# Up-projection of three batches as seven block products with reloaded weights, down-projection in groups, and an order made by a list scheduler

## The chip, the cores and the metric

The kernel runs on one core of one Trainium2 chip. The time is device microseconds (us) of one execution. A core has TensorE (PE, matrix products, with its weight loads PEld counted apart), VectorE (DVE), ScalarE (ACT), GpSimd (POOL) and SyncE (SP, which here issues the transfers between DRAM and the on-chip memory SBUF). Products accumulate in PSUM, in banks of 128 x 512 f32. "L523" is a line of the kernel file.

## The reference

Four batches of 768 tokens, 8 heads of 64. Each query sees the keys less than 16 places away and 24 further keys, each the maximum of a block of 32 keys; their scores get log 32 added and their values are the blocks' means. The 512 numbers per token then go through a gated layer:

```
k_sum = k.reshape(B, H, nb, block, D).max(axis=3)
v_sum = v.reshape(B, H, nb, block, D).mean(axis=3)
...
x = attn_out.transpose(0, 2, 1, 3).reshape(B * S, H * D)      # 3072 x 512
g = x @ w_gate                                                # 512 x 1536
silu = g * (1.0 / (1.0 + np.exp(-g)))
val = x @ w_val
return (silu * val @ w_out).astype(np.float32)                # 1536 x 512
```

The three weight matrices come as float64 and are made into f32 on the chip by integer operations.

## The kernel before, in words

Tokens are worked on in 8 blocks k of 384 (batch k // 2, half k % 2). Attention is done in units (k, u), u = 0 to 3 being a pair of heads: scores on PE (L404), maximum on DVE (L419), exponential on ACT (L434), reciprocal on DVE (L454), scaling on POOL or DVE (L458), transposes on PE (L473), copies on ACT or DVE, values on PE (L497, tile xo). The unit's output, transposed, is 128 rows of x for 384 tokens, and `a_split` keeps it as a high part xh and a low part xl. Every f32 product of the gated layer is three matmuls in a fast format: low weight by high x, high weight by low x, high by high.

d_ff is cut into 12 slices j of 128. `m_up(k, j, nm)` makes gate or value of a block and slice: 4 row blocks u by 3 matmuls of 128 x 128 by 384 columns (L523). Then come silu on ACT (L530), the product with the value on DVE (L535, tile a), its high part ah on ACT (L159) and low part al on POOL or DVE (L155). `m_down(k, j)` is 9 matmuls of 512 columns (L574: 3 token tiles by 3 terms) into three PSUM banks, in which all 12 slices add up; after the last, three copies and stores (L581).

Weights: `w_load` (L175) fetches 1 MB of gate and value for a slice (gv) or 0.5 MB of w_out (o); `w_abs` (ACT, L184, the magnitude), `w_clamp`, `w_shift`, `w_sign` and `w_low` (DVE, L191 to L211) make f32 from the two words of a float64; `w_hi` (L159, ACT) and `w_lo` (L155, DVE or POOL) split it into the high and low part. The split weights of all 12 slices stay in SBUF to the end: every weight is loaded and decoded once.

The order of the work in blocks 0 and 1 is a text written by hand (`PROLOGUE`), with the engine of some steps in it; then a loop over (k, j) has gate, value and the down-projection of the slice before it, and attention of the next block is put at fixed places of the loop. On each engine, the instructions are chained in the order in which they were written.

## Time and profile before

| | us |
|---|---|
| three timed runs | 716.29, 717.04, 717.61 (median 717.04) |
| span of the profiled execution | 715.0 |
| PE busy in it | 704.7 (5062 instructions) |
| ACT, DVE, POOL busy | 322.2, 283.6, 140.1 |
| first gate product starts | 36.0 |
| last matmul ends | 711.25 |
| read from DRAM, written | 54.93 MB, 6.29 MB |

Group rows read: line, engine, operation, output<-inputs by the program's names, shape, count, then busy us in all and ns of one, then the engine's idle time ahead of them and who ended it. In the chain of waits each row is a start, a length, and the work or the wait that held the end at that time. A stretch's row has its length, the busy us and counts of PE, PEld, DVE, ACT and POOL, the granted clock of PE (1.00 is full speed), the busy share of the DMA engines and GB/s. A transfer's row has its size and the median us from issue to landing.

### The profile page before, as it was taken

To read this page: it belongs to the slowest core of one execution; us is meant where nothing else is said; L and a number is where in the kernel's file an instruction comes from. 1 tells how busy PE (TensorE), PEld (TensorE's weight loads), DVE (VectorE), ACT (ScalarE), POOL (GpSimd) and SP (SyncE) were. 2 spreads that over 40 slices of the span, in tenths; PEclk is the share of its full clock that TensorE was granted. 3 is DMA by queue.
4 is the path that set the end of the run, shared out by engine and by line. 5 is a ranking of instruction groups with operands and counts; after the bars stand their busy time and mean duration, and the time that the engine had idled before them with its cause. 6 is when DMAs were issued, how large, how long until landed. Compare 5 with 4: busy or idle time off the path is not lost.

```text
span 715.0 us, 12684 instructions
## 1 busy us (share of the span) xinstructions
PE 704.7 (99%) x5062; PEld 644.5 (90%) x5062; DVE 283.6 (40%) x832; ACT 322.2 (45%) x782; POOL 140.1 (20%) x155
## 2 busy tenths in 40 slices
PE   8899999999999999999999999999999999999997
PEld 7688999999889999999999999999999999999996
DVE  5999999926553212323422222232222321210001
ACT  5998444314774434544434444343444433421111
POOL 3232000002222122222122222122222212211111
PEclk9999999999999999999999999999999999999999
DMA  9999400407553101223213211111111200010001
GB/s 301 335 370 382 101 1 1 130 1 220 164 161 111 43 3 45 90 68 90 78 42 106 67 45 45 45 61 30 45 45 45 89 17 1 1 45 1 0 1 45
DMA packets 56523, 62.04 MB, mean 87 GB/s; under 512 B 24272, under 2 KB 46480, under 8 KB 55184
## 3 DMA queue, kind: packets, MB, share of 16 engines
q1 hardware_dynamic: 56464, 61.23, 27.4%
q8 instruction: 40, 0.66, 0.4%
q14 instruction: 19, 0.16, 0.1%
HBM read 54.93 MB, written 6.29 MB: 86 GB/s over the span
## 4 chain that ended last, share of the span: by engine, by line
PE 91%; DMA 4%; ACT 3%; issue 1%; SPq 0%; DVE 0%; ACTq 0%
PE v L523 28%; PE acc L574 27%; PE g L523 27%; PE xo L497 4%; PE sc L404 3%; PE pp L473 2%; DMA vw<-in_vP 1%; ACT p L434 1%; DMA raw_g<-in_wgv 1%; DMA kt<-in_kP 1%; ACT pt L159 0%; PE pv L373 0%; ACT L434 0%; ACT L530 0%; DVE m_gv L211 0%
## 5 line engine op out<-in xcount | busy, mean ns | idle before, releaser
L574 PE MATMUL acc<-w_o,ah 128*128 128x512 f32 x576 | 179.3, 392 | 0.0
L523 PE MATMUL v<-xh,w_gv 128*128 128x384 f32 x640 | 179.1, 340 | 0.0
L523 PE MATMUL g<-xh,w_gv 128*128 128x384 f32 x640 | 178.0, 339 | 0.0
L535 DVE TENSOR_TENSOR a<-v,a 128x384 f32<-128x384 f32 x96 | 53.3, 555 | 255.5 <-PE v L523 255.3
L155 POOL TENSOR_TENSOR al<-a,ah 128x384 fp32r<-128x384 f32 x79 | 81.1, 1027 | 264.5 <-ACT ah L159 264.5
L574 PEld LDWEIGHTS acc<-w_o,ah 128*128 128x128 f32 x576 | 108.0, 188 | 20.1
L523 PEld LDWEIGHTS v<-xh,w_gv 128*128 128x128 f32 x640 | 117.0, 188 | 3.1 <-issue 2.4
L523 PEld LDWEIGHTS g<-xh,w_gv 128*128 128x128 f32 x640 | 117.2, 188 | 2.9 <-issue 0.2
L574 PE MATMUL acc<-w_o,al 128*128 128x512 f32 x288 | 114.2, 396 | 0.0
L530 ACT ACTIVATE a<-g 128x384 f32<-128x384 f32 x96 | 47.1, 491 | 144.6 <-PE g L523 144.3
L523 PE MATMUL g<-xl,w_gv 128*128 128x384 f32 x320 | 107.8, 337 | 0.0
L523 PE MATMUL v<-xl,w_gv 128*128 128x384 f32 x320 | 107.7, 337 | 0.0
L159 ACT CAST ah<-a 128x384 fp32r<-128x384 f32 x92 | 46.9, 510 | 112.1 <-DVE a L535 112.1
L434 ACT ACTIVATE p<-p,nm 128x120 f32<-128x120 f32 x192 | 73.3, 383 | 1.1 <-DVE nm L419 0.7
L574 PEld LDWEIGHTS acc<-w_o,al 128*128 128x128 f32 x288 | 54.0, 188 | 10.1 <-issue 0.5
L523 PEld LDWEIGHTS g<-xl,w_gv 128*128 128x128 f32 x320 | 60.1, 188 | 2.5
L523 PEld LDWEIGHTS v<-xl,w_gv 128*128 128x128 f32 x320 | 60.1, 188 | 0.0
L530 ACT ACT_TABLE_LOAD x27 | 34.6, 1283 | 52.7 <-PE g L523 52.6
L458 POOL TENSOR_TENSOR p<-p,ri 128x720 f32<-128x720 f32 x26 | 36.2, 1391 | 98.5 <-DVE ri L454 98.0
L419 DVE CUSTOM_DVE_ANT_0 p<-sc,bias_sb 128x120 f32<-128x120 f32 x192 | 41.4, 276 | 0.7 <-PE sc L404 0.7
L523 PE MATMUL v<-xh,w_v 128*128 128x384 f32 x128 | 36.1, 342 | 0.7 <-DVE w_v L155 0.7
L523 PE MATMUL g<-xh,w_g 128*128 128x384 f32 x128 | 36.1, 343 | 0.0
(103 smaller groups left out, 721.3 us busy)
## 6 DMA issues: line engine op xcount, KB each, us to landing
raw_gv<-in_wgv SPq DMA_DIRECT2D x10, 1024.0 KB, 12.8
kw<-in_kP SPq DMA_DIRECT2D x28, 288.0 KB, 4.1
vw<-in_vP SPq DMA_DIRECT2D x28, 288.0 KB, 3.4
q<-in_qP SPq DMA_DIRECT2D x32, 192.0 KB, 3.6
raw_o<-in_wo SPq DMA_DIRECT2D x12, 512.0 KB, 11.5
out<-o SPq DMA_DIRECT2D x24, 256.0 KB, 2.3
stg<-in_kP SPq DMA_DIRECT2D x12, 400.0 KB, 3.7
vt<-in_vT SPq DMA_DIRECT2D x12, 384.0 KB, 3.5
```

Of the source, the lines that this page charges most:

```text
L155: (nc.vector if e == "d" else nc.gpsimd).tensor_tensor(out=out, in0=a, in1=b.bitcast(F32), op=ALU.subtract)
L159: nc.scalar.copy(out, in_)
L404: nc.tensor.matmul(sc[h][s * QT : (s + 1) * QT, c * KC : (c + 1) * KC], t["q"][hs, qs], t["kw"][hs, i, :], start=True, stop=True,)
L419: nc.vector.tensor_tensor_reduce(out=t["p"][:, i, :], in0=t["sc"][g][:, c * KC : (c + 1) * KC], in1=bias_sb[:, 0 if n == 0 else 2 if n == ...
L434: nc.scalar.activation(out=t["p"][:, i, :], in_=t["p"][:, i, :], func=AF.Exp, scale=-1.0, bias=t["nm"][:, i : i + 1], accum_out=t["sm"][:, ...
L458: (nc.vector if on == "d" else nc.gpsimd).tensor_tensor(out=p, in0=p, in1=ri.rearrange("p (n o) -> p n o", o=1).broadcast_to([P, NT, KC]), ...
L473: nc.tensor.transpose(ps[:KC, c * P : (c + 1) * P], U[k, u]["p"][:, g * NT // 2 + c, :], id_sb)
L497: nc.tensor.matmul(ps[hs, qs], vw, t["pt"][:, h, qs], start=True, stop=True)
L523: nc.tensor.matmul(ps[:, :TOK], w[:, cs], x, start=u == 0 and n == 0, stop=u == NP - 1 and n == 2)
L530: nc.scalar.activation(out=a, in_=A.pop(("g", k, j))[:, :TOK], func=AF.Silu)
L535: nc.vector.tensor_tensor(out=a, in0=ps[:, :TOK], in1=a, op=ALU.mult)
L574: nc.tensor.matmul(ACC[k][i], a[:, ts], w, start=j == 0 and n == 0, stop=j == NJ - 1 and n == 2)
```

## The change: seven block products, sums of weights, groups, and a scheduler

**Seven products.** For batches 1 to 3 the 512 rows of x are cut into two halves and the 768 tokens into two: blocks B11, B12, B21, B22 (row half, token half). For a slice j, gate weights are A11, A12 and value weights A21, A22 (by row half). With S1 = A21 + A22, S3 = A11 - A21, S2 = S1 - A11, S4 = A12 - S2 and T1 = B12 - B11, T2 = B22 - T1, T3 = B22 - B12, T4 = B21 - T2, the products P1 = A11 B11, P2 = A12 B21, P3 = S4 B22, P4 = A22 T4, P5 = S1 T1, P6 = S2 T2, P7 = S3 T3 give gate and value of both halves: gate of half 0 is P1 + P2; with U = P1 + P6, value of half 0 is U + P7 + P4, gate of half 1 is U + P5 + P3, value of half 1 is U + P5 + P7. Each product is 2 row blocks by 3 matmuls of 384 columns (`product`). P2, P4 and P3 are accumulated in the banks of P1, P7 and P5, after these have been copied or read (`s1`, `s7`, `v`); the rest is added on DVE and POOL.

**Operands.** `x_operands(b)` makes the seven high and low pairs from the batch's x: 8 subtractions, and a cast and a subtraction for each of 14 tiles. Attention units of batches 1 to 3 leave x as f32 (`a_keep`).

**Weights.** Batch 0 decodes the slices as before (`w_first`), now in a ring of four SBUF slots, and stores the split weights in DRAM (`wa{j}`, 1 MB each). In batches 1 to 3 `w_next` loads, for each slice, the three blocks that are used as they are, and the sums. In batch 1 the sums are made: the whole slice is loaded again, high and low added (`sm`), four sums made (`sums`), split (`sh`, `sl`), and stored (`ss{j}`); batches 2 and 3 load these. w_out stays in SBUF.

**Down-projection.** In groups of three slices: 9 matmuls for each and each of the six token tiles of a batch, in one bank; the group's sum is copied into (first group) or added to an f32 tile in SBUF (`part`), from which the output is stored.

**Order.** A `Plan` collects steps with the buffers that they read and write, the engines that can do them, and a cost for each. `order` simulates the engines, with a lag after PE and transfers, a price for a change of ACT's table, and gives each step an engine and a place; steps of attention go on a second list of PE's work, which is taken when the main one waits or when its time comes. The instructions are then chained in that order.

```diff
-    def m_up(k, j, nm):
-        ps = spare(psg.tile([P, 512], F32, tag="b", name=f"{nm}_{k}_{j}"))
-        wh, wl = W[nm, j]
-        for u in range(NP):
-            xh, xl = X[k, u]
-            cs = slice(u * P, (u + 1) * P)
-            for n, (w, x) in enumerate(((wl, xh), (wh, xl), (wh, xh))):
-                nc.tensor.matmul(
-                    ps[:, :TOK], w[:, cs], x, start=u == 0 and n == 0, stop=u == NP - 1 and n == 2
-                )
...
-            terms = ((al, wh), (ah, wl), (ah, wh)) if k < NBLK - 1 else ((ah, wh), (ah, wl), (al, wh))
-            for n, (a, w) in enumerate(terms):
-                nc.tensor.matmul(
-                    ACC[k][i], a[:, ts], w, start=j == 0 and n == 0, stop=j == NJ - 1 and n == 2
-                )
...
-    for n, (k, j) in enumerate(seq):
-        m_gate(k, j)
-        do(3 * n)
-        m_val(k, j)
-        do(3 * n + 1)
-        if prev:
-            m_down(*prev)
-        do(3 * n + 2)
-        prev = (k, j)
-    m_down(*prev)
...
+LAG = {PE: 0.28, DMA: 1.9}
+TABLE = 1.3
+SLACK = 2.5
+EARLY = 6.0
+BIAS = {DVE: 1.2, ACT: 0.6}
...
+    def x_operands(b):
+        for kk in range(2):
+            b11, b12, b21, b22 = XF[b, kk, 0], XF[b, kk, 1], XF[b, 2 + kk, 0], XF[b, 2 + kk, 1]
+            t3 = buf("late", f"t3{kk}", [P, TOK], f"t3_{b}_{kk}", room="late")
+            x_sum(b, "T3", kk, t3, b22, b12)
+            x_sum(b, "T1", kk, b12, b12, b11)
+            x_operand(b, "B11", kk, b11)
+            x_sum(b, "T2", kk, b11, b22, b12)
+            x_operand(b, "T3", kk, t3)
+            x_operand(b, "T1", kk, b12)
+            x_operand(b, "T2", kk, b11)
+            x_operand(b, "B21", kk, b21)
+            x_sum(b, "T4", kk, b21, b21, b11)
+            x_operand(b, "T4", kk, b21)
+            x_operand(b, "B22", kk, b22)
...
+    def split(name, w, m, n, engines=(DVE, POOL)):
+        hi, lo = lambda: make(w)[:, 0], lambda: make(w)[:, 1]
+        add_copy(f"hi {name}", (ACT,), n, hi, lambda: make(m), (m,), ((w, 0),))
+        plan.add(
+            f"lo {name}", on(engines, "tt", n), lambda e: minus(e, lo(), make(m), hi().bitcast(F32)), (m, (w, 0)), ((w, 1),)
+        )
...
+    def w_next(b, j):
+        wa = buf("wts", slot(), [P, 2, NC - HALF], f"wa_{b}_{j}", F32R)
+        add_dma(f"la({b},{j})", P * NC * 6, lambda: make(wa).bitcast(F32), lambda: make(WA[j])[:, :, HALF:], (WA[j],), (wa,))
+        s = buf("wts", slot(), [P, 2, NC], f"s_{b}_{j}", F32R)
+        if b == 1:
+            hi, lo = lambda: make(s)[:, 0], lambda: make(s)[:, 1]
+            add_dma(f"ls({b},{j})", P * NC * 8, lambda: make(s).bitcast(F32), lambda: make(WA[j]), (WA[j],), (s,))
+            cols = {x: slice(i * HALF, (i + 1) * HALF) for i, x in enumerate(("A21", "A11", "A12", "A22"))}
+            m = buf("tmp", "m", [P, NC], f"m_{b}_{j}", room="tmp")
+            at = lambda x: make(m)[:, cols[x]]
+            plan.add(
+                f"sm({j})", on((DVE, POOL), "tt", NC),
+                lambda e: tt(e, make(m), lo().bitcast(F32), hi().bitcast(F32), ALU.add), (s,), (m,),
+            )
+            def sums(e):
+                tt(e, at("A22"), at("A21"), at("A22"), ALU.add)
+                minus(e, at("A21"), at("A11"), at("A21"))
+                minus(e, at("A11"), at("A22"), at("A11"))
+                minus(e, at("A12"), at("A12"), at("A11"))
+            plan.add(f"sums w{j}", {POOL: 2.9, DVE: 1.7}, sums, (), (m,))
+            add_copy(f"sh({j})", (ACT, DVE), NC, hi, lambda: make(m), (m,), ((s, 0),))
+            plan.add(
+                f"sl({j})", on((DVE, POOL), "tt", NC), lambda e: minus(e, lo(), make(m), hi().bitcast(F32)), (m, (s, 0)), ((s, 1),)
+            )
+            ss = SS[j] = buf("dram", f"ss{j}", [P, 2, NC], f"ss{j}")
+            add_dma(f"ss({j})", P * NC * 8, lambda: make(ss), lambda: make(s).bitcast(F32), (s,), (ss,))
+        else:
+            add_dma(f"ls({b},{j})", P * NC * 8, lambda: make(s).bitcast(F32), lambda: make(SS[j]), (SS[j],), (s,))
+        W[b, j] = (wa, s)
...
+    def product(b, j, name, weight, xname, acc, first, last):
+        wa, s = W[b, j]
+        ops = [X[b, xname, kk] for kk in range(2)]
+        src, at = {
+            "A11": (wa, 0), "A12": (wa, 1), "A22": (wa, 2), "S3": (s, 0), "S2": (s, 1), "S4": (s, 2), "S1": (s, 3),
+        }[weight]
+        def do(e):
+            t = make(acc)
+            warm_up(t)
+            for kk in range(2):
+                xh, xl = (make(x) for x in ops[kk])
+                c = at * HALF + kk * P
+                wh, wl = (make(src)[:, i, c : c + P] for i in range(2))
+                for n, (a, x) in enumerate(((wl, xh), (wh, xl), (wh, xh))):
+                    nc.tensor.matmul(
+                        t[:, :TOK], a, x, start=first and kk == 0 and n == 0, stop=kk == 1 and n == 2,
+                        skip_group_check=not first,
+                    )
+        plan.add(f"{name}({b},{j})", {PE: 6 * 0.1755}, do, [src] + sum(ops, []), (acc,))
...
+    def u_seven(b, j):
+        tmp = lambda name: buf("tmp", name, [P, TOK], f"{name}_{b}_{j}", room="tmp")
+        p1, p7, p5, p6 = (bank("m", f"{x}_{b}_{j}") for x in ("p1", "p7", "p5", "p6"))
+        of = lambda x: lambda: make(x)[:, :TOK]
+        full = lambda x: lambda: make(x)
+        product(b, j, "P1", "A11", "B11", p1, True, False)
+        s1 = tmp("s1")
+        add_copy(f"s1({b},{j})", (ACT, DVE), TOK, full(s1), of(p1), (p1,), (s1,), kind="evict")
+        product(b, j, "P7", "S3", "T3", p7, True, False)
+        s7 = tmp("s7")
+        add_copy(f"s7({b},{j})", (ACT, DVE), TOK, full(s7), of(p7), (p7,), (s7,), kind="evict")
+        product(b, j, "P5", "S1", "T1", p5, True, False)
+        v = tmp("v")
+        add_tt(f"v({b},{j})", (DVE,), TOK, full(v), of(p5), full(s7), ALU.add, (p5, s7), (v,))
+        product(b, j, "P6", "S2", "T2", p6, True, True)
+        u2 = tmp("u2")
+        add_tt(f"u2({b},{j})", (DVE,), TOK, full(u2), of(p6), full(s1), ALU.add, (p6, s1), (u2,))
+        product(b, j, "P2", "A12", "B21", p1, False, True)
+        a = [buf("x", f"a{hf}", [P, TOK], f"a_{b}_{j}_{hf}") for hf in range(2)]
+        silu(f"silu({b},{j},0)", a[0], of(p1), (p1,))
+        product(b, j, "P4", "A22", "T4", p7, False, True)
+        c21 = s1
+        add_tt(f"c21({b},{j})", (DVE,), TOK, full(c21), of(p7), full(u2), ALU.add, (p7, u2), (c21,))
+        add_tt(f"mul({b},{j},0)", (DVE, POOL), TOK, full(a[0]), full(c21), full(a[0]), ALU.mult, (c21,), (a[0],))
+        hidden(b, j, 0, a[0])
+        c22 = v
+        add_tt(f"c22({b},{j})", (POOL, DVE), TOK, full(c22), full(v), full(u2), ALU.add, (v, u2), (c22,))
+        product(b, j, "P3", "S4", "B22", p5, False, True)
+        c12 = u2
+        add_tt(f"c12({b},{j})", (DVE,), TOK, full(c12), of(p5), full(u2), ALU.add, (p5, u2), (c12,))
+        silu(f"silu({b},{j},1)", a[1], full(c12), (c12,))
+        add_tt(f"mul({b},{j},1)", (DVE, POOL), TOK, full(a[1]), full(c22), full(a[1]), ALU.mult, (c22,), (a[1],))
+        hidden(b, j, 1, a[1])
+    PART = {}
...
+        def finish():
+            if g == 0:
+                part = PART[t] = buf("late", f"part{t}", [P, DM], f"part_{b}_{t}", room="late")
+                add_copy(f"part({b},{g},{t})", (ACT, DVE), DM, lambda: make(part), lambda: make(acc), (acc,), (part,), kind="evict")
+            else:
+                part = PART[t]
+                add_tt(f"part({b},{g},{t})", (DVE,), DM, lambda: make(part), lambda: make(acc), lambda: make(part), ALU.add, (acc,), (part,))
+            if g == NJ // GROUP - 1:
+                r = b * S + t * P
+                add_dma(f"out({b},{t})", P * DM * 4, lambda: out[r : r + P, :], lambda: make(part), (part,), ())
+        return [lambda n=n: piece(n) for n in range(len(pieces))], finish
...
+    units(1, 0.0, 10.0, 1.5)
+    for j in range(4, NJ):
+        w_first(j)
+        if j == 4:
+            o_first(3)
+        o_first(j)
+        for hf in range(2):
+            spend(lambda: u_plain(j, hf))
+        if j % GROUP == GROUP - 1:
+            if j == NJ - 1:
+                plan.mark("tmp", "dec", lambda: (close_pool("dec"), open_pool("tmp", side="right", reuse_waits="tile")))
+            for n in range(2):
+                spend(lambda: downs(0, j // GROUP, range(3 * n, 3 * n + 3)))
+    while todo:
+        todo.pop(0)[2]()
+    for b in range(1, B):
+        x_operands(b)
+        clock[0] = 0.0
+        if b + 1 < B:
+            units(b + 1, 4.0, 14.5)
+        for j in range(NJ):
+            w_next(b, j)
+            spend(lambda: u_seven(b, j))
+            if j % GROUP == GROUP - 1:
+                for n in range(2):
+                    spend(lambda: downs(b, j // GROUP, range(3 * n, 3 * n + 3)))
+        while todo:
+            todo.pop(0)[2]()```

Two places where the order of the instructions differs. In the rows: line of the file, operation, output<-inputs with the names of the tiles (their last number is a running one), shape.

ACT before the first gate product. Before, `m_g0` is the decoded gate half of slice 0, `w_g0` its split form, `pt` the transposed probabilities of a unit (k, u):

```order
L184 ACTIVATE m_g0_355<-raw_g0_280 128x512
L159 COPY vw_0_1_312<-vs_0_259 24x384
L159 COPY vn2_122<-vs_0_259 24x3x128
L159 COPY vn0_220<-vs_0_259 24x3x128
L159 COPY pt_0_3_397<-pp1_0_3_366 120x384
L434 ACTIVATE p_0_2_385,sm_0_2_387<-p_0_2_385,nm_0_2_386 128x120 x6
L159 COPY pt_0_0_453<-pp1_0_0_434 120x384
L159 CAST xh_0_3_458<-xo_0_3_408 128x384
L184 ACTIVATE m_gv1_466<-raw_gv1_331 128x1024
L159 CAST w_g0_482<-m_g0_355 128x512
```

The same place after the change, with `m_w0` for the whole slice 0, gate and value, and `m_o0`, `m_o1` for slices 0 and 1 of w_out:

```order
L747 ACTIVATE m_w0_447<-raw_w0_239 128x1024
L330 COPY pt_0_0_445<-pp1_0_0_441 120x384
L747 ACTIVATE m_w1_457<-raw_w1_256 128x1024
L330 COPY pt_0_2_479<-pp0_0_2_462 120x384
L330 COPY pt_0_2_479<-pp1_0_2_475 120x384
L747 ACTIVATE m_o0_501<-raw_o0_449 128x512
L330 CAST xh_B11_0_0_503<-xo_0_0_484 128x384
L747 ACTIVATE m_o1_519<-raw_o1_459 128x512
L330 CAST xh_B21_0_0_524<-xo_0_2_505 128x384
L330 CAST w0_534<-m_w0_447 128x1024
```

Between the magnitude of slice 0 and its cast there now stand the magnitudes of a whole slice more and of two slices of w_out.

DVE in batch 1, at the end of slice 1 and the sums of slice 2. `s_1_2` is the slot with slice 2's weights (batch, slice), `m_1_2` the f32 tile of its sums, `v`, `u2`, `s1`, `s7` are the partial sums of slice 1, `hh` and `hl` the high and low parts of the hidden values (batch, slice, half), `p_4_0` unit 0 of block 4:

```order
L332 CAST hh_1_0_1_2979<-a_1_0_1_2935 128x384
L332 COPY s7_1_1_2981<-p7_1_1_2954 128x384
L335 TENSOR_TENSOR v_1_1_2994<-p5_1_1_2972,s7_1_1_2981 128x384
L335 TENSOR_TENSOR u2_1_1_3005<-p6_1_1_2985,s1_1_1_2964 128x384
L335 TENSOR_TENSOR m_1_2_3011<-s_1_2_2951 128x1024
L335 TENSOR_TENSOR s1_1_1_2964<-p7_1_1_2954,u2_1_1_3005 128x384
L496 TENSOR_SCALAR sm_4_0_2968<-sm_4_0_2968 128x6
L499 RECIPROCAL ri_4_0_3049<-sm_4_0_2968 128x6
L335 TENSOR_TENSOR u2_1_1_3005<-p5_1_1_2972,u2_1_1_3005 128x384
L502 TENSOR_TENSOR p_4_0_2944<-p_4_0_2944,ri_4_0_3049 128x720
```

Joining slice 2's high and low (`m_1_2`) stands between the partial sums of slice 1; before, DVE had one operation for a half and slice between its attention work.

POOL at the same place, after the change:

```order
L335 TENSOR_TENSOR v_1_1_2994<-v_1_1_2994,u2_1_1_3005 128x384
L335 TENSOR_TENSOR m_1_2_3011<-m_1_2_3011 128x256 x4
L335 TENSOR_TENSOR a_1_1_0_3025<-s1_1_1_2964,a_1_1_0_3025 128x384
L335 TENSOR_TENSOR a_1_1_1_3053<-v_1_1_2994,a_1_1_1_3053 128x384
L332 COPY kw_4_3_3084<-ks_2_3_2289 128x6x24
L335 TENSOR_TENSOR hl_1_1_0_3089<-a_1_1_0_3025,hh_1_1_0_3080 128x384
L335 TENSOR_TENSOR hl_1_1_1_3103<-a_1_1_1_3053,hh_1_1_1_3087 128x384
```

Where a slice had two low parts before, one for each half, there are now five operations and the four sums.

More of the change, by code (lines that the diff above doesn't have):

```diff
@@ L124, with cost @@
-"""
-def read_steps(text):
-    for step in text.split():
-        call, _, engines = step.partition("=")
-        name, _, args = call.partition("(")
-        yield name, [int(x) if x.isdigit() else x for x in args[:-1].split(",") if x], engines
+PE, DVE, ACT, POOL, DMA = "PE", "d", "a", "p", "q"
+def cost(e, kind, n):
+    if kind == "copy":
+        return {DVE: 0.12 + 0.0006 * n, ACT: 0.11 + 0.00098 * n, POOL: 0.09 + 0.00108 * n}[e]
+    if kind == "evict":
+        return {DVE: 0.155 + 0.00104 * n, ACT: 0.11 + 0.00098 * n}[e]
+    if kind == "scalar":
+        return 0.15 + 0.00052 * n
+    return {DVE: 0.155 + 0.00108 * n, POOL: 0.13 + 0.00235 * n}[e]
@@ new lines, with order @@
+LAG = {PE: 0.28, DMA: 1.9}
[3 more added lines that the diff above has]
+BIAS = {DVE: 1.2, ACT: 0.6}
+def order(steps):
+    for s in steps:
+        s.next = []
+    for s in steps:
+        for o in s.after:
+            o.next.append(s)
+    pe = [s for s in steps if PE in s.engines]
+    line = [[s for s in pe if s.side == x] for x in range(2)]
+    wanted = {}
+    t = 6.0
+    for s in pe:
+        wanted[s] = t
+        t += s.engines[PE]
+    for _ in range(3):
+        late = {}
+        for s in reversed(steps):
+            x = wanted.get(s, 1e9)
+            for o in s.next:
+                x = min(x, late[o] - (LAG.get(o_engine(s), 0.12) if s.after is not None else 0))
+            late[s] = x - min(s.engines.values(), default=0)
+        run(steps, line, late)
+        wanted = {s: s.start + s.engines[PE] for s in pe}
+        for s in line[1]:
+            if s.gate is not None:
+                wanted[s] = min(wanted[s], s.gate.end + EARLY)
+    return sorted(steps, key=lambda s: (s.start, s.n))
@@ new lines, in downs, with warm_up @@
+    def downs(b, g, ts):
+        made = [down(b, g, t, True) for t in ts]
+        for i in range(0, len(ts), 3):
+            some = made[i : i + 3]
+            for n in range(2):
+                for pieces, finish in some:
+                    pieces[n]()
+                    if n == 1:
+                        finish()
+    def warm_up(ps):
+        for _ in range(spare[0]):
+            nc.tensor.matmul(ps[:, TOK:], make(warm), make(warm), start=True, stop=True)
+        spare[0] = 0
+    warm = buf("dec", "warm", [P, P], "warm")
@@ L708, in body @@
[L708 to L722 removed]
+            a_load_value_rows(b, u)
+            a_pool_keys(b, u)
+            a_pool_values(b, u)
@@ new lines, in body @@
+    last = {}
+    for s in order(plan.steps):
+        if s.engine == PE and s.start < 60.0:
+            spare[0] = min(10, max(0, int((s.idle - 0.5) / 0.25)))
+        n = len(traced)
+        if s.engine is None:
+            s.do()
+        else:
+            s.do(s.engine)
+        spare[0] = 0
+        for x in traced[n:]:
+            if x.engine in last:
+                after(x, last[x.engine])
+            last[x.engine] = x
+    for name in list(pools)[::-1]:
+        close_pool(name)
```

1197 lines of the change are left out of this document (702 added, 495 removed).

## The prediction, on record before the result

> **What bounds the kernel now.** I read the page first, then the chain of waits, then the stretches of the span.
>
> ```profile
> span 715.0 us, 12684 instructions
> ...
> PE 704.7 (99%) x5062; PEld 644.5 (90%) x5062; DVE 283.6 (40%) x832; ACT 322.2 (45%) x782; POOL 140.1 (20%) x155
> ...
> PE 91%; DMA 4%; ACT 3%; issue 1%; SPq 0%; DVE 0%; ACTq 0%
> ```
>
> PE works in nearly all of the 715.0 us of the profiled execution; the others have between 393 and 575 us left. The chain of waits tells the same, and gives the price of work on PE, since in it one matmul follows another without a gap (columns: start us, us on the chain, what):
>
> ```profile
> 58.88 0.84 PE sc L404 x22
> ...
> 62.85 2.11 PE g L523 x12
> 64.96 2.11 PE v L523 x12
> 67.06 0.66 PE pp L473 x6
> 67.72 2.08 PE acc L574 x9
> 69.80 0.85 PE xo L497 x24
> ...
> 704.92 2.08 PE v L523 x12
> 707.00 4.25 PE acc L574 x18
> ```
>
> An up-projection matmul (384 columns) takes 2.11/12 = 0.176 us on the chain early and 2.08/12 = 0.173 late; I use 0.1755. A down-projection matmul takes 2.08/9 = 0.231. The means of single matmuls in the groups overlap (below: 392 ns for a down matmul that takes 231 of the chain) and must not be added.
>
> ```profile
> L574 PE MATMUL acc<-w_o,ah 128*128 128x512 f32 x576 | 179.3, 392 | 0.0
> ```
>
> The last matmul ends at 711.25, and 3.7 us of copy and store follow. Stretch by stretch (after the range: length, then busy us and count of PE, PEld, DVE, ACT, POOL; granted clock, DMA share, GB/s):
>
> ```profile
> 0.00:20.00 20.00, 17.43 (x216) 14.75 (x217) 12.49 (x57) 11.24 (x44) 6.50 (x17) 1.00 0.95 309
> 20.00:40.00 20.00, 17.12 (x236) 14.18 (x235) 19.02 (x69) 19.63 (x61) 6.83 (x7) 1.00 0.97 343
> 80.00:140.00 60.00, 60.00 (x316) 56.09 (x315) 59.23 (x95) 26.02 (x39) 1.30 (x1) 1.00 0.13 40
> 200.00:620.00 420.00, 420.00 (x3055) 385.72 (x3054) 114.10 (x421) 184.78 (x460) 93.64 (x98) 1.00 0.20 57
> ```
>
> The gate products by their line (count, durations, first and last start):
>
> ```profile
> L523 PE MATMUL g<-xh,w_g x128: 331/336/445, 36.0 to 704.6; 128*128 128x384 f32 x128
> ```
>
> From 200 on PE has no gap at all; before 40 the attention of the first block and the decoding of the weights set the pace, with DMA 95% busy, and the first gate product starts at 36.0 (the first number after the durations). So a matmul that is removed after 40 is worth its whole time, as long as what feeds PE keeps up. That is the whole question here: PE has no slack, and the change puts more on every other engine.
>
> **The gain on PE.** Before, a batch and a slice j of d_ff take 2 halves x 24 = 48 up matmuls; seven products of 6 are 42. In all 2304 become 576 (batch 0, as before) + 3 x 12 x 42 = 1512, so 2088. The 864 down matmuls and the 32 attention units stay. 216 x 0.1755 = **-37.9 us** (-37.4 by the late price). 715.0 - 37.9 = 677.1. A product now has 6 matmuls in a row instead of 12, 252 against 72 x 2 = 144 in these batches. If each change of product cost the 2.11 - 2.08 = 0.03 us by which the early row is dearer, that were 108 x 0.03 = 3; the late rows change bank at the same places and show nothing, so I take 0.
>
> **The start, +7.** Batch 0 now goes j by j for both halves, with whole slices of 1 MB. The order on ACT puts the magnitudes of o0 and o1 ahead of the cast of w0, the first one that a gate product needs. Their prices:
>
> ```profile
> raw_gv<-in_wgv SPq DMA_DIRECT2D x10, 1024.0 KB, 12.8
> raw_o<-in_wo SPq DMA_DIRECT2D x12, 512.0 KB, 11.5
> ...
> L159 ACT CAST w_gv<-m_gv 128x1024 fp32r<-128x1024 f32 x10 | 10.5, 1048 | 5.7 <-DVE m_gv L211 5.6
> ...
> L155 DVE TENSOR_TENSOR w_gv<-m_gv,w_gv 128x1024 fp32r<-128x1024 f32 x8 | 9.7, 1215 | 0.7 <-ACT w_gv L159 0.7
> ...
> L155 POOL TENSOR_TENSOR w_gv<-m_gv,w_gv x2: 2397/2404/2410, 35.9 to 60.1; 128x1024 fp32r<-128x1024 f32 x2
> ```
>
> o1's transfer is the 26th that SP issues, and those before it and itself carry about 10.9 MB by their shapes. At the 309 and 343 GB/s of the rows above these land near 34; then its magnitude, the cast of w0 (1.05) and the low part on POOL (2.4): first gate at about 38.5, +2.5. Next, unit (1,3)'s scores, softmax and values stand ahead of the second half's products, and slice 2's decoding ahead of its first half; I put 2 and 2.5 on these two. Bounds: 2.5 (only the first) to 13 (both waits doubled and the transfers another 1.5 late). I take +7, nearer the rows than their double.
>
> **The weight sums in batch 1, +12.** For each j two slots are loaded: three blocks as they are (0.79 MB), and the whole slice (1.05 MB), from which four sums are made in place and stored. A slot comes free after the last product of j-2, and the sums are wanted at the second product of j. The row of an SBUF load of near size, and of the subtraction on POOL:
>
> ```profile
> stg<-in_kP SPq DMA_DIRECT2D x12, 400.0 KB, 3.7
> ...
> L155 POOL TENSOR_TENSOR al<-a,ah 128x384 fp32r<-128x384 f32 x79 | 81.1, 1027 | 264.5 <-ACT ah L159 264.5
> ```
>
> The load: 3.7 + 0.62 MB at 343 GB/s = 5.6 in a quiet queue, 12.8 in the crowded one of the start; batch 1 moves 2.9 MB and attention's 0.77 MB in 13.3 us, 276 GB/s, less than the start's 309 to 343, so I take 6.0. Then joining high and low on DVE 1.2, four sums of 256 columns on POOL (4 x 256/384 x 1.03 = 2.8), cast on ACT 1.05, low part on DVE 1.2, five hand-overs of 0.12: 6.0 + 6.25 + 0.6 = 12.85. Against it PE has 42 x 0.1755 = 7.4 of j-1, one product of j (1.05) and attention of about 1.3 (scores 0.84, transposes 0.66 and values 0.85 a unit by the chain, so a little more than half a unit): 9.7. Where the downs of a group (6 x 9 x 0.231 = 12.5) lie between, which is so for j = 3, 4, 6, 7, 9, 10, the chain is hidden. For j = 2, 5, 8, 11 it isn't: 4 x 3.1 = **+12**. Bounds: the quiet load and two units of attention as filler leave 1 each (+4); a load of 12.8 leaves 9.9 each (+39). I take the middle price because the queue's rate lies between these rows and nearer the quiet one. In batches 2 and 3 the sums only have to be loaded: 6 against 9.7, hidden; at 12.8 with two thirds of the traffic it isn't, but no row after 140 shows such a queue.
>
> The Trainium skill, page "TensorE: Matmul & The Clock Gate", section "HAM oscillation — how this bites in real kernels", says that PE idle for more than about 3.4 us falls back to half clock, some 1.7 us a time. The stretches above have a granted clock of 1.00 throughout, and no idle time that long after the start, so no run here shows it; by that rule the four waits, if a little longer than I think, would cost some 3 us more (an estimate: 4 x 1.7, half of it lost).
>
> **Other work off PE.** Each j of batches 1 to 3 has two evictions, three sums on PSUM, one more add and the two multiplications, most on DVE and POOL; each group adds into SBUF. The rows of the same kinds before:
>
> ```profile
> L535 DVE TENSOR_TENSOR a<-v,a 128x384 f32<-128x384 f32 x96 | 53.3, 555 | 255.5 <-PE v L523 255.3
> ...
> L530 ACT ACTIVATE a<-g 128x384 f32<-128x384 f32 x96 | 47.1, 491 | 144.6 <-PE g L523 144.3
> ...
> L159 ACT CAST ah<-a 128x384 fp32r<-128x384 f32 x92 | 46.9, 510 | 112.1 <-DVE a L535 112.1
> ...
> L161 DVE COPY o<-acc 128x512 f32<-128x512 f32 x8 | 5.5, 691 | 9.3 <-PE acc L574 9.3
> ```
>
> With the counts of the new order times such rows (DVE 0.555 and POOL 1.03 at 384 columns, 0.69 for a group's sum) DVE comes to some 376 us of the span, ACT 306, POOL 339: none is the bound as a sum. After the last product of a group j, 0.57 + 0.49 + 1.03 + 0.51 + 1.03 = 3.6 us go by until its low part is there; the downs of the two earlier j (3 x 6 x 0.231 = 4.2) lie ahead, so nothing. If that cover were gone it would be 3.6 x 9 = 33. Borders between batches (22 subtractions and 14 casts into the operands): the last downs (12.5) cover all but the first products' operands, **+2** (0 to 8). The slices' copies to DRAM in batch 0 cost PE nothing by themselves.
>
> DVE and POOL together are another matter. Four rows of the start, in which both work on SBUF alone:
>
> ```profile
> 44.13 1.22 DVE L204 SCALAR_TENSOR_TENSOR m_gv<-raw_gv,m_gv 128x1024 int32<-128x1024 int32 x1
> 44.20 2.01 POOL L155 TENSOR_TENSOR al<-a,ah 128x384 fp32r<-128x384 f32 x1 [5.46 <-ACT ah L159]
> ...
> 54.45 2.05 DVE L204 SCALAR_TENSOR_TENSOR m_gv<-raw_gv,m_gv 128x1024 int32<-128x1024 int32 x1
> ...
> 54.13 1.29 POOL L155 TENSOR_TENSOR w_o<-m_o,w_o 128x512 fp32r<-128x512 f32 x1 [6.88 <-issue]
> ```
>
> The POOL subtraction that began while DVE was at work took 2.01, not 1.03; the DVE operation that began in POOL's took 2.05, not 1.30. The one waits for the other to end. In batches 0 and 1 there are now some 195 such operations on DVE and 172 on POOL (1.14 us each on average). Expected wait: POOL is at it in 54% of the time, half an operation is left, 195 x 0.54 x 0.57 = 60 us on DVE. DVE's own work there is 253 us of the roughly 360 from the first gate product to the end of batch 1, so 313 of 360: it fits, with late decodings now and then, **+4** (0 to 22, the latter is the third rival).
>
> **The sum.** 677.1 + 7 + 12 + 4 + 2 = 702.1 us of span. The timed runs (median 717.04) lie 2.0 above the profiled span of 715.0: **704 us**. Its own range, with the start between 5 and 9, the sums between 6 and 18, the ports between 0 and 6: 694 to 712.
>
> **Rivals.**
>
> *PE stays full (25%).* The order was made from a list with prices close to those above; if attention fills the four waits and the ports collide seldom, only the start is late: 677.1 + 7 + 2.0 = 686. For it: 200 to 620, where PE never waited, with POOL 22% and DVE 27% busy. Against it: 12.85 against 9.7 by rows.
>
> *Late loads (10%).* SP issues in order, and the store of the sums of j stands among the loads of j+1 and j+2. If a load of batch 1 lands half way between quiet and crowded, 9.4, each of the four waits grows by 3.4: 702.1 + 13.6 + 2.0 = 718. For it: the crowded rows. Against it: 276 GB/s is less than the queue has carried, and six of twelve slices have the downs as cover.
>
> *DVE and POOL block each other until DVE is the bound (15%), the one that ends slower.* Place: batches 0 and 1. DVE has 360 - 253 = 107 us to lose there, so it decides from 107/195 = 0.55 us per operation on. At 0.66 (POOL's 1.14, held in 58% of the cases because a blocked DVE and a busy POOL queue up behind each other) DVE needs 253 + 129 = 382, 22 more than there is: 702.1 - 4 + 22 + 2.0 = 722, and with the sums' own chain, whose three steps on these two engines then wait 0.6 each (4 x 1.8 = 7), 729. I take 725. For it: the rows at 44 and 54. Against it: 60 us is what independent times give, and operations that read PSUM are not of this kind. The Trainium skill, page "SBUF — State Buffer", section "Who interferes with whom", calls this an exclusive lock on a shared port pair: the second one is fully blocked. The four rows agree; that rule sets no price of its own here.
>
> **How the numbers follow.** Forecast 50%, PE full 25%, late loads 10%, DVE and POOL 15%. 8 times in 10: from 684 (PE full, with 2 us less at the start) to 720 (late loads); this leaves out the case of 725 and a little below. A measurement of this kernel tells 0.2% (1.4 us) from no change. Faster: the forecast, PE full and nearly all of late loads (718 is near the edge, I count half), 0.50 + 0.25 + 0.05 = 0.80. Same: a piece of late loads and of the ports, 0.05. Slower: 0.15.
>
> **What would show it.** Up products x2088, and in batches 2 and 3 no gap on PE: 37.9 us less busy. First gate near 38.5. In batch 1 four idle stretches of PE near 3 us, released by the low part of the sums, at j = 2, 5, 8, 11 and nowhere else. The clock at 1.00. POOL's subtractions with a tail at 2 us. If the waits stand at every j, or PE's idle time lies in batch 0, released by decodings, or at the downs, the forecast is wrong; so it is if up matmuls take more than 0.176 us on the chain.

## The result, and the profile after

The changed kernel takes 749.46 us (median of four runs, 748.9 to 751.36) against 717.33: the ratio is 1.0456, with a 95% interval of 1.0438 to 1.0474. It is slower by 32 us where the prediction had it faster by 13. The profiled execution's span is 747.0. From the page of the changed kernel:

```profile
span 747.0 us, 13223 instructions
...
PE 693.5 (93%) x4886; PEld 623.1 (83%) x4886; DVE 475.9 (64%) x1022; ACT 372.3 (50%) x864; POOL 389.7 (52%) x369
...
PEclk9989999899999999989999899999999999999999
...
PE 60%; DVE 22%; DMA 8%; issue 6%; POOL 2%; SPq 1%; ACT 1%; DVEq 0%; ACTq 0%; POOLq 0%
```

PE has 176 instructions fewer (216 matmuls removed, 40 added by dummies, which are matmuls without a use that fill idle time of PE), but of the chain that ended last only 60% is PE's now, and 22% DVE's. The clock row has digits under 9 that the kernel before doesn't have. The waits of PE say on whom:

```profile
PE p L890 <- DVE s L335: 18.0, 4, 6.4
PE sc L450 <- DVE nm L467: 5.1, 1, 5.1
PE acc L950 <- DVE part L335: 4.6, 3, 2.5
PE pp L523 <- POOL p L502: 4.2, 4, 2.7
```

(waiting line, releaser: us in total, times, longest.) The first row is the four waits for the low part of the weight sums. By stage (stretches from the first product of a batch to that of the next; columns as before):

```profile
43.00:254.00 211.00, 195.07 (x1438) 172.52 (x1439) 178.12 (x352) 128.60 (x288) 113.81 (x92) 0.95 0.63 214
254.00:443.00 189.00, 168.89 (x1161) 151.13 (x1161) 133.29 (x277) 99.83 (x225) 113.78 (x104) 0.95 0.70 239
443.00:606.00 163.00, 160.45 (x1155) 143.80 (x1154) 86.69 (x225) 90.92 (x213) 85.47 (x83) 0.99 0.53 177
606.00:747.00 141.00, 137.19 (x723) 128.19 (x721) 50.65 (x84) 33.56 (x70) 53.88 (x52) 1.00 0.41 148
```

The loss is in batches 0 and 1, where POOL is busy for 114 us each and the mean clock is 0.95. With the prices of the prediction (0.1755 and 0.231 us a matmul, 2.55 us an attention unit: from 36.0 to 711.25 less the 2304 and 864 matmuls at these prices, 71.3 us are left for 28 units) the predicted 702.1 falls into these parts:

| part | predicted | measured | difference |
|---|---|---|---|
| first gate product | 38.5 | 43.1 | +4.6 |
| batch 0 | 190 | 211.3 | +21 |
| batch 1 | 171 | 188.3 | +17 |
| batch 2 | 160 | 163.7 | +4 |
| batch 3 and tail | 143 | 140.5 | -2.5 |

### The profile page after: what moved, and what is told of

Same layout as the page of the kernel before. It is cut to its first block, busy times and chain, and to the rows that moved or that the text cites. A ratio compares the mean times of both kernels' runs of the same rounds, so it can differ in the third digit from the quotient of the medians.

```text
span 747.0 us, 13223 instructions
## 1 busy us (share of the span) xinstructions
PE 693.5 (93%) x4886; PEld 623.1 (83%) x4886; DVE 475.9 (64%) x1022; ACT 372.3 (50%) x864; POOL 389.7 (52%) x369
## 4 chain that ended last, share of the span: by engine, by line
PE 60%; DVE 22%; DMA 8%; issue 6%; POOL 2%; SPq 1%; ACT 1%; DVEq 0%; ACTq 0%; POOLq 0%
PE p L890 31%; PE acc L950 19%; DMA s<-wa 3%; PE v L867 2%; PE g L867 2%; PE xo L554 2%; PE sc L450 2%; DVE a L335 2%; PE pp L523 2%; DVE s L335 1%; DVE xl_B L335 1%; DVE m_w L764 1%; SPq L349 1%; DVE p L467 1%; DVE m_w L751 1%
## 5 line engine op out<-in xcount | busy, mean ns | idle before, releaser
L950 PE MATMUL acc<-o,hh 128*128 128x512 f32 x576 | 185.9, 404 | 7.2 <-DVE part L335 4.6
L890 PE MATMUL p<-xh_T,s 128*128 128x384 f32 x432 | 125.5, 354 | 18.7 <-DVE s L335 18.0
L335 POOL TENSOR_TENSOR hl<-a,hh 128x384 fp32r<-128x384 f32 x92 | 107.1, 1170 | 58.0 <-ACT hh L330 36.2
L950 PEld LDWEIGHTS acc<-o,hh 128*128 128x128 f32 x576 | 105.5, 191 | 31.9 <-DVE part L335 5.9
L950 PE MATMUL acc<-o,hl 128*128 128x512 f32 x288 | 114.3, 397 | 1.6 <-POOL hl L335 1.6
L890 PEld LDWEIGHTS p<-xh_T,s 128*128 128x128 f32 x432 | 83.5, 199 | 20.7 <-DVE s L335 19.0
L890 PE MATMUL p<-xh_B,wa 128*128 128x384 f32 x288 | 86.6, 341 | 0.0
L335 POOL TENSOR_TENSOR v<-v,u 128x384 f32<-128x384 f32 x33 | 34.4, 1042 | 96.5 <-DVE u L335 89.5
L890 PE MATMUL p<-xl_T,s 128*128 128x384 f32 x216 | 75.2, 348 | 0.0
L335 DVE TENSOR_TENSOR part<-acc,part 128x512 f32<-128x512 f32 x72 | 48.4, 687 | 40.2 <-PE acc L950 40.1
L950 PEld LDWEIGHTS acc<-o,hl 128*128 128x128 f32 x288 | 54.8, 190 | 14.9 <-POOL hl L335 2.9
L502 POOL TENSOR_TENSOR p<-p,ri 128x720 f32<-128x720 f32 x27 | 38.3, 1420 | 47.8 <-DVE ri L499 43.7
L867 PE MATMUL g<-xh_B,w 128*128 128x384 f32 x192 | 57.4, 361 | 3.4 <-POOL w L335 2.7
L335 DVE TENSOR_TENSOR v<-p,s 128x384 f32<-128x384 f32 x36 | 20.0, 556 | 58.4 <-PE p L890 51.0
L867 PE MATMUL v<-xh_B,w 128*128 128x384 f32 x192 | 55.3, 349 | 0.0
L330 ACT COPY s<-p 128x384 f32<-128x384 f32 x61 | 29.1, 478 | 52.0 <-PE p L890 51.3
L890 PEld LDWEIGHTS p<-xh_B,wa 128*128 128x128 f32 x288 | 53.1, 188 | 1.6 <-issue 0.8
L330 ACT CAST hh<-a 128x384 fp32r<-128x384 f32 x65 | 33.1, 511 | 42.4 <-DVE a L335 31.4
L467 DVE CUSTOM_DVE_ANT_0 p<-sc,bias_sb 128x120 f32<-128x120 f32 x192 | 41.6, 276 | 17.3 <-PE sc L450 16.7
L335 POOL TENSOR_TENSOR a<-s,a 128x384 f32<-128x384 f32 x32 | 33.3, 1040 | 32.3 <-DVE s L335 25.0
```

Source lines behind the costliest of these rows:

```text
L330: nc.scalar.copy(out, in_)
L335: vector[e].tensor_tensor(out=out, in0=a, in1=b, op=op)
L467: nc.vector.tensor_tensor_reduce(out=make(p)[:, i, :], in0=make(sc[g])[:, c * KC : (c + 1) * KC], in1=make(bias_sb)[:, 0 if n == 0 else 2 ...
L502: vector[e].tensor_tensor(out=make(p), in0=make(p), in1=make(ri).rearrange("p (n o) -> p n o", o=1).broadcast_to([P, NT, KC]), op=ALU.mult,)
L867: nc.tensor.matmul(t[:, :TOK], a, x, start=u == 0 and n == 0, stop=u == NP - 1 and n == 2)
L890: nc.tensor.matmul(t[:, :TOK], a, x, start=first and kk == 0 and n == 0, stop=kk == 1 and n == 2, skip_group_check=not first,)
```

## The experiments

Times are medians; "batch 0" and the like are the lengths from first product to first product in that run's trace, which is of one execution. Where the order is that of the changed kernel, batch 0 took 211.3 (changed kernel), 212.8 (run 1), 213.7 (run 3) and 216.6 (run 4), so a difference of some us between two such lengths can be chance. The kernel before took 716.4 to 717.3 beside these runs.

**1. The weight sums left out.**

```diff
-            add_dma(f"ls({b},{j})", ..., lambda: make(SS[j]), (SS[j],), (s,))
+            add_dma(f"ls({b},{j})", ..., lambda: make(WA[j]), (SS[j],), (s,))
...
+        elif s.name[:3] in ("sm(", "sum", "sh(", "sl(", "ss("):
+            continue
```

> Leaves the making of the weight sums out: in all of batches 1 to 3 the slice's split weights are loaded in their place (products with them are wrong), and the joining, the four sums, their split and their store are gone; the order of all that is left is the same. Theory 1 (the chain of load and sums is longer than one slice of PE's work): the four waits at j = 2, 5, 8, 11 of batch 1 (18.0 us) go, since a load of 7.8 us alone is shorter than 9.7, and with them the half clock behind them (20.5 us at half speed, 10.2 lost): 749.5 - 28 = 721, within 4. Rival (DVE and POOL as a whole are too slow in batch 1, the sums are only where it shows): about 10 us less, 739, and waits at other places of batch 1. Batch 0 (211 us) unchanged in both.

723.84, ratio 1.0086 (1.0068 to 1.0105). Batch 1 takes 162.2, batches 2 and 3 are as they were, and the row of PE's waits for the sums is gone. So the sums are worth 26 us. But this takes their work and their wait away together.

**2. A third slot for the sums, all work kept.**

```diff
-        s = buf("wts", slot(), [P, 2, NC], f"s_{b}_{j}", F32R)
+        tag = ("w4", "w3", "w0")[n % 3]
+        s = buf("tmp" if tag == "w4" else "wts", tag, [P, 2, NC], f"s_{b}_{j}", F32R, ...)
```

> All work kept, but the sums have three slots and the plain blocks two, so a load of sums waits for the products of three slices before, not two; the order is made anew by the scheduler. Theory 1: the chain starts 7.4 us or more earlier and is hidden, as in the run without sums: 721, within 5. Rival: the sums' work itself on DVE and POOL costs the time, whenever it starts: waits move, 735 to 749. Batch 0 unchanged.

748.65: nothing gained in the whole; batch 1 is 4.4 us shorter (183.9) and batch 0 4.3 longer (215.6). The theory fell in this form. PE's waits in this run:

```profile
PE acc L953 <- DVE part L335: 8.3, 3, 3.1
PE sc L450 <- DVE nm L467: 6.6, 1, 6.6
PE acc L953 <- POOL hl L335: 5.6, 5, 2.2
PE g L870 <- DVE w L335: 5.0, 1, 5.0
...
PE p L893 <- DVE s L332: 3.5, 2, 3.3
```

The waits for the low part of the weight sums (18.0) are gone, and others take their place, for DVE and POOL above all. The last row is a copy of a partial sum (L332) that DVE makes only after weight sums (2.54 us for the last three) and the cast of a high part (1.40). An earlier load doesn't help while these two engines are behind.

**3 and 4. The clock: dummy matmuls in the idle times**, first too many, then sized.

```diff
+        spare[0] = {"PP0(2,3)": 11, "P7(1,2)": 19, "P7(1,5)": 28, "P7(1,8)": 15,
+                    "P7(1,11)": 17, "D0(2,3,5)": 11}.get(s.name, spare[0])     # first: 22, 40, 57, 30, 35, 22, and 24 at g(0,0)
```

> Nothing changed but dummy matmuls (128 x 128 by 128 columns) in PE's idle time, ahead of g(0,0), of a transpose of unit (2,3), of the second product at j = 2, 5, 8, 11 of batch 1, and of the last down-projection of group 3 of batch 2; their number fills each idle time at 0.11 us each. Theory 2 (PE idle for some 2.5 us or more is followed by 3.4 or 6.8 us at half clock): the stretches at half clock go from 44.4 us to the some 10 after the idle times that are left, so 15 to 17 us less: 733. Rival (the low clock has another cause than the idle time, as the power of denser work): the same stretches at half clock, 749 or a little more.

> As the run with dummies, but sized by what that run showed: a dummy is two matmuls of some 0.1 us each, so 0.22 us apiece, and 11, 19, 28, 15, 17 and 11 of them stand ahead of the transpose of unit (2,3), the second product at j = 2, 5, 8, 11 of batch 1, and the down-projection at the end of batch 2. They fill those idle times and no more. Theory 2 (idle time brings half clock): the six stretches at half clock behind these places (27.3 us of 44.4) are gone, worth 13.7 us: 735, within 4. Rival (the dummies only move the low clock, or cost what they save): 745 to 752.

768.66 and 747.75. In both, the stretches at half clock in batch 1 are gone; the first kernel's dummies took twice their place, since each is two matmuls in the trace, and it says nothing of the price. The second, around the first and the second of the four waits, beside the changed kernel:

```profile
275.00:285.00 10.00, 9.85 (x90) 9.38 (x87) 8.68 (x23) 6.97 (x17) 9.76 (x10) 1.00 0.91 306
...
320.00:340.00 20.00, 20.00 (x174) 18.87 (x173) 16.85 (x32) 14.33 (x33) 16.77 (x17) 1.00 0.82 260
```

```profile
270.00:280.00 10.00, 5.63 (x47) 4.77 (x46) 8.67 (x22) 6.68 (x12) 8.71 (x9) 0.90 0.81 282
...
320.00:330.00 10.00, 3.64 (x55) 3.09 (x55) 9.90 (x13) 4.08 (x7) 7.97 (x7) 0.79 0.75 252
330.00:340.00 10.00, 10.00 (x49) 9.38 (x49) 6.44 (x22) 8.10 (x19) 8.32 (x9) 0.87 0.69 202
```

So the idle time brings the half clock. Its price was put too high: batch 1 is 5.1 us shorter in this trace, not 10.2. The whole is only 1.7 us shorter, which lies in the rival's range. In the trace batch 0 is 5.3 us longer, with a wait of 5.0 us at 61, ahead of the first added dummy, where the changed kernel's trace has 0.57. A stretch doesn't cost half of its length, since those of the longer waits begin while PE still waits: the second one goes from 325.8 to 332.6, and the first matmul in it starts at 328.3. Matmuls that start in a stretch are 0.32 us apart, not 0.174; counted so, all nine stretches cost about 17 us and those of batch 1 about 7.

**5. Less work on POOL in batch 0**, the same order: no low parts of hidden values and w_out, no scaling.

```diff
+                    al = make(HH[b, j, hf][1])[:, cs] if b else ah
+                    wh = wl = make(O[j])[:, 0]
...
+        elif s.name[:4] in ("lo o", "hl(0") or left and s.engine == POOL and s.name[:3] == "nrm":
+            continue
```

> In batch 0, POOL leaves out the low parts of the hidden values, of w_out, and the scaling of the probabilities (65 of its some 92 us between the first gate product and 235); the products take the high part in their place, the same number of matmuls, the order is the same. Theory 3 (POOL's operations on SBUF hold up those of DVE, some 33 us in batch 0, and DVE is what PE waits for there): DVE's shift and mask operations on 512 columns go back from 774 and 1168 ns towards 413 and 683, batch 0 is 10 to 18 us shorter (part of it clock): 735, within 5. Rival (DVE's own work in batch 0 is too much, whoever is beside it): batch 0 at most 4 us shorter, 746.

735.88, and batch 0 takes 197.4, 13.9 us less. The edit also takes away PE's waits for POOL's own results, but from the first gate product on these were only 1.7 us of batch 0. Two of DVE's decoding operations on 512 columns, in the kernel before, in the changed one and here:

```profile
L211 DVE SCALAR_TENSOR_TENSOR m_o<-raw_o,m_o 128x512 int32<-128x512 int32 x12 | 8.0, 683 | 0.0
...
L196 DVE TENSOR_SCALAR m_o<-m_o 128x512 int32<-128x512 int32 x12 | 5.0, 413 | 0.0
```

```profile
L770 DVE SCALAR_TENSOR_TENSOR m_o<-raw_o,m_o 128x512 int32<-128x512 int32 x12 | 14.0, 1168 | 0.1
...
L757 DVE TENSOR_SCALAR m_o<-m_o 128x512 int32<-128x512 int32 x12 | 9.2, 774 | 0.1
```

```profile
L770 DVE SCALAR_TENSOR_TENSOR m_o<-raw_o,m_o 128x512 int32<-128x512 int32 x12 | 10.2, 849 | 0.1
...
L757 DVE TENSOR_SCALAR m_o<-m_o 128x512 int32<-128x512 int32 x12 | 7.3, 612 | 0.1
```

**6. Batch 1 plain**, as batch 0, with the sums made behind the slice's products for batches 2 and 3.

```diff
+            if b == 1:
+                w_again(j)
+                spend(lambda: u_plain(j, 0, 1))
+                spend(lambda: u_plain(j, 1, 1))
+                w_sums(j)
+            else:
+                w_next(b, j)
+                spend(lambda: u_seven(b, j))
```

> Batch 1 is computed as batch 0, with 24 matmuls for a half and slice, from whole slices loaded again; the weight sums are still made there, but after the slice's products, for batches 2 and 3 alone, so nothing in batch 1 waits for them. PE has 72 matmuls more, 12.6 us. Theory 1 in the form that the first runs leave (in batch 1 the sums' work, seven-product work and attention together are more than DVE and POOL do in time): batch 1 takes 158.4 + 12.6 + 3 = 174 where it took 188: 735, within 5. Rival (the sums' work costs the same wherever it is done, about 20 us): batch 1 at 190 or more: 750.

736.90; batch 1 takes 175.1, with 72 matmuls (12.6 us) more than in the changed kernel, where it took 188.3. That is the 162.2 of run 1 and 12.6. The sums are made in full, and as long as no product waits for them they cost nothing that shows.

**7. Third slot and less POOL in batches 0 and 1.** The edits of 2 and 5, the latter up to the end of batch 1.

> Third slot for the sums, and POOL leaves out the low parts of the hidden values (batches 0 and 1), of w_out, and the scaling of the probabilities up to the end of batch 1, as in the run with less POOL; the products take the high part. All sums are made. Theory 3 (POOL's operations hold up DVE's in batch 1 too): batch 0 at 197 us as in that run, batch 1 at 165 to 170 where the third slot alone had 184: 720, within 5. Rival (in batch 1 it is the order and the sums' own length): batch 1 at 180 or more: 733.

718.49 (ratio 1.0023, 1.0006 to 1.0039). Batch 1 takes 165.9, where the third slot alone had 183.9 and POOL's relief of batch 0 alone 189.8. So in batch 1 too POOL's work is what keeps the sums late once they have the slot; less POOL in batch 1 without the slot was not run. Batch 0 is at 204.3, not 197: its order was made anew.

**8 and 9. The ports in the scheduler's plan.** All work is kept. The plan holds an operation of DVE on SBUF alone back while one of POOL's runs, and the other way round; copies of the pooled values go to ACT, low parts of weights to DVE, and `BIAS`, which is added to an engine's cost when one is chosen, falls to 0 for ACT and rises to 0.6 for POOL, so that POOL gets less. `SLACK` and `EARLY`, which bear on when attention's matmuls are taken, move too. First all of it with batch 1 plain; then, with batch 1 plain too, the lock alone (of the edit below only the `port` lines):

```diff
+        if held(e, s):
+            start = max(start, port[0])
...
+            port[0] = s.end
...
-BIAS = {DVE: 1.2, ACT: 0.6}
+BIAS = {DVE: 1.2, ACT: 0, POOL: 0.6}
-EARLY = 6.0
+EARLY = 10.0
-SLACK = 2.5
+SLACK = 1.0
```

> All work kept. Batch 1 plain with the sums on the side; and the scheduler is told that an operation of POOL and one of DVE on SBUF alone do not run at once, with copies of the values on ACT, low parts of weights on DVE, and its weights for the choice of an engine moved so that POOL gets less. Theory 3: with this, batch 0 falls from 211 to 190 to 200 and batch 1 to 174, with fewer stretches at half clock: 716, within 8. Rival (the ports are not what delays batch 0; DVE has more to do in this version): batch 0 stays at 211 or gets longer: 735 or more.

> Batch 1 plain, and the scheduler told of the ports, but copies, low parts and the weights for the choice of an engine left as in the change: what the order alone gives. If the order is what matters: near 706. If it is how much POOL is given (its busy time falls from 390 to 278 us in the run with both): most of the 34 us between 737 and 703 stays: 728, within 6.

703.06 with all of it (ratio 0.9816, 0.9791 to 0.984) and 723.62 with the lock in the plan alone. Of the 33.8 us from 736.9 the lock gives 13.3. The other 20.6 come with giving POOL less (busy 278 us; 359 with the lock alone, 357 without it) and with `SLACK` and `EARLY`, which were not moved by themselves; in the two traces 5.7 of them lie ahead of the first gate product and 11.5 in batch 0. Batch 0 falls to 192.7 (204.2 with the lock alone), and from 140 on PE has no gap:

```profile
140.00:240.00 100.00, 100.00 (x777) 89.51 (x779) 77.42 (x166) 64.88 (x147) 31.51 (x28) 1.00 0.59 205
240.00:400.00 160.00, 160.00 (x1179) 147.20 (x1176) 96.84 (x227) 106.77 (x221) 72.65 (x64) 1.00 0.61 208
```

**10 and 11. The change in full, with that plan,** with two slots and with three.

> The change as it is, all its work with the seven products in batch 1 and two slots for the sums; only the scheduler is told of the ports and its choice of engines moved, as in the run with the lock in the plan. Theory 3 and 1 together: batch 0 at 193 as there, batch 2 at 158, and batch 1 still has its four waits of some 3 to 4.5 us with half clock behind them, some 178: 715, within 6. Rival (what that run gained it gained from the plain batch 1): 735 or more.

> As the change with the ports in the plan, and the third slot for the sums. Theory 1 in its last form (the waits for the sums are the chain's once DVE and POOL have room): batch 1 at 163 to 170, total 704, within 6, about that of the plain batch 1. Rival (the third slot does as little as it did alone, 4 us): 711 or more.

721.16 and **701.33** (ratio 0.9781, 0.975 to 0.9813), faster than the kernel before and than the changed one. Batch 0 takes 190.3 and 189.6, batch 2 157.7 in both; batch 1 takes 185.3 with two slots (I expected 178) and 166.6 with three. The slot that gave 4 us alone gives 19 now. (With two slots the executions ran from 714.9 to 724.4, and the traced one is the 714.9.) The stages of the last one:

```profile
42.00:231.00 189.00, 185.37 (x1438) 165.84 (x1437) 164.06 (x364) 142.88 (x314) 65.73 (x54) 1.00 0.73 244
231.00:398.00 167.00, 161.61 (x1159) 144.61 (x1159) 131.73 (x267) 107.96 (x246) 117.14 (x101) 0.99 0.79 269
398.00:556.00 158.00, 158.00 (x1160) 143.78 (x1159) 80.15 (x218) 98.32 (x231) 73.04 (x71) 1.00 0.54 183
```

POOL's 114 us in batch 0 have become 66, and DVE's 178 have become 164, though DVE took low parts over from POOL: what DVE was busy with had partly been waiting.

**12. The kernel before, with idle work on POOL.** Nothing of the change, but 48 subtractions that nobody reads, while DVE decodes (two behind each of 24 casts; 50 were expected).

```diff
         copy(on or "a", hi, m)
+        for i in range(2):
+            nc.gpsimd.tensor_tensor(out=idle[0], in0=hi.bitcast(F32)[:, :384], in1=hi.bitcast(F32)[:, :384], op=ALU.subtract)
```

> The kernel before, with 50 subtractions of 128x384 added on POOL between some 40 and 140 us, where DVE is full: two behind each cast of a weight's high part, reading it and writing a tile that nobody reads. Theory 3 (one of POOL's and one of DVE's operations on SBUF exclude each other): DVE's decoding operations are held up, by 25 to 50 us in all, their means on 512 columns rise from 413 and 681 ns as in the changed kernel; the decoding ends at 160 to 185 where it ended at 141, and what PE loses is what of that the decoded slices in stock don't cover: 0 to 25 us, 717 to 742. Rival (no such lock): DVE's means as before, decoding over at 141, 717.

739.62 (ratio 1.0318, 1.0303 to 1.0333). DVE from 46 to 200, before and here, and the added work on POOL (its largest group):

```profile
L155 DVE TENSOR_TENSOR w_o<-m_o,w_o 128x512 fp32r<-128x512 f32 x9 | 6.1, 682 | 0.2 <-ACT w_o L159 0.2
...
L196 DVE TENSOR_SCALAR m_o<-m_o 128x512 int32<-128x512 int32 x11 | 4.5, 413 | 0.0
```

```profile
L156 DVE TENSOR_TENSOR w_o<-m_o,w_o 128x512 fp32r<-128x512 f32 x10 | 11.8, 1183 | 0.0
...
L197 DVE TENSOR_SCALAR m_o<-m_o 128x512 int32<-128x512 int32 x11 | 6.9, 627 | 0.0
...
L224 POOL TENSOR_TENSOR idle<-w_o 128x384 f32<-128x384 f32 x24 | 28.7, 1195 | 21.5 <-ACT w_o L160 20.2
```

Some 60 us of work that has no reader makes a kernel 23 us slower. DVE's busy time rises by 27.0 us (283.6 to 310.6) with the same 832 instructions. Not all of the 23 need be that: from 36 on PE's waits end with DVE for 13.9 us and with POOL for 4.8, where a copy or a low part that PE needs stands behind the added subtractions, and two stretches of 3.41 us at half clock come on top.

## Why the prediction was wrong

**The gain on PE: right.** Batches 2 and 3, where the sums are only loaded, are within 4 us of their predicted lengths, and with the ports in the plan batch 2 takes 157.7. The 37.9 us are there; 70 were lost elsewhere (32 + 37.9): 43 is more idle time of PE (53.5 us, the span less its busy time, against 10.3), about 17 half clock, and some 10 are left that no view puts in one place (the 40 matmuls of dummies are among them).

**The ports, "+4": the step that failed.** The expected wait itself was about right: I put DVE at 313 us in batches 0 and 1, 60 of them waits, and it was busy for 311 (178.1 and 133.3); by the means the four decoding operations alone lost 25 us in batch 0. What was wrong is "313 of 360: it fits". It summed two batches, while the decoding has to be done slice by slice in the first one:

```profile
100.00:110.00 10.00, 6.81 (x22) 4.91 (x23) 10.00 (x9) 3.79 (x5) 5.89 (x4) 0.87 0.24 97
120.00:140.00 20.00, 14.89 (x91) 14.06 (x90) 19.96 (x45) 14.80 (x38) 11.03 (x10) 0.83 0.75 247
```

DVE is full there, PE waits, and there is nothing to catch up with. The longest wait of batch 0, 5.11 us, ends with attention's maxima (L467); ahead of them DVE has a decoding operation of 2.67 us, 0.683 in the kernel before, beside one of POOL's:

```profile
126.14 2.67 DVE L770 SCALAR_TENSOR_TENSOR m_o<-raw_o,m_o 128x512 int32<-128x512 int32 x1
128.74 0.27 DVE L467 CUSTOM_DVE_ANT_0 p<-sc,bias_sb 128x120 f32<-128x120 f32 x1
```

```profile
125.90 2.36 POOL L335 TENSOR_TENSOR w<-m_w,w 128x1024 fp32r<-128x1024 f32 x1 [2.29 <-ACT w L330]
```

So batch 0 took 21 us more than its forecast with the +4 in it, half clock behind the waits included. Run 5 takes 13.9 of them back by leaving out work of POOL, and runs 8, 10 and 11, with the ports in the plan and less given to POOL, bring the batch to 190 to 193, where the forecast had 190. The kernel before has DVE full too in these stretches (59.23 of 60 us from 80 to 140), but POOL at 1.3 us. The third rival had the mechanism, and "slower", with 15%; its 725 was still 24 too low, and its condition (0.55 us lost per operation over both batches) was the wrong one. That it is POOL, and not the amount of DVE's work, is shown by runs 5 and 12 and agrees with run 8, in which DVE took over low parts.

**The weight sums, "+12": right in place, too small.** The four waits stand at j = 2, 5, 8, 11, as forecast, and are 18.0 instead of 12.4. The one at j = 5, from the landing of the load on, on DVE and POOL, and the product that waited:

```profile
319.34 1.23 DVE L335 TENSOR_TENSOR m<-s 128x1024 f32<-128x1024 f32 x1 [1.84 <-DMA s<-wa]
...
322.80 1.21 DVE L502 TENSOR_TENSOR p<-p,ri 128x720 f32<-128x720 f32 x1
323.93 1.07 DVE L335 TENSOR_TENSOR a<-v,a 128x384 f32<-128x384 f32 x1
325.04 1.31 DVE L332 CAST hh<-a 128x384 fp32r<-128x384 f32 x2
326.27 2.01 DVE L335 TENSOR_TENSOR s<-m,s 128x1024 fp32r<-128x1024 f32 x1
```

```profile
320.64 3.95 POOL L335 TENSOR_TENSOR m<-m 128x256 f32<-128x256 f32 x4 [1.76 <-DVE m L335]
```

```profile
328.33 0.69 PE L890 MATMUL p<-xh_T,s 128*128 128x384 f32 x1 [6.36 <-DVE s L335]
```

The four sums took 3.95, not 2.8, the low part 2.01, not 1.2, with other operations ahead of it, and the load 7.66 from issue to landing, not 6.0 (7.1 is the median of the twelve). So each of these terms was mis-sized. The two on DVE and POOL grew beside operations of the other engine, as in batch 0: from 326.16 on POOL was at two subtractions (2.98 us). That a longer load alone isn't it is shown by run 2; that the chain matters once the two engines have room, by runs 10 and 11.

**The clock: left out of the sum.** The Trainium skill, page "TensorE: Matmul & The Clock Gate", section "HAM oscillation — how this bites in real kernels", was quoted with some 3 us (an estimate) for the four waits; those of batch 1 cost about 7. The trace agrees that idle time of PE brings the half clock. It differs in the length, 3.41 or 6.83 us at a time where the Trainium skill has some 1.7, and in the condition, since waits of 2.1 to 2.7 us were enough. The nine stretches, 44.4 us in all, cost about 17. A rule that speaks against the change should have been given the idle time of the pessimistic cases.

**The start, "+2.5": right in kind, 4.6 too small.** ACT waits for o1 ahead of the cast of w0, as forecast, but o1 lands at 38.1, not 34:

```profile
38.12 0.68 ACT L747 ACTIVATE m_o<-raw_o 128x512 f32<-128x512 f32 x1 [0.88 <-DMA raw_o<-in_wo]
```

The two further waits that I put there (4.5) are 0.57 and 0.76 us in this trace; the first is 3.5 in that of run 1 and 5.0 in that of run 4, in the same order.

**Downs, borders, other work: right**, as far as it goes: a wait of 2.5 us before the last downs of batch 2; of 8.8 us at downs in all, 4.6 are for the groups' sums on DVE.
